# Second MLP of a three-stage kernel: a cast deferred into the next group, last blocks of the first MLP pulled forward, weight conversion reordered

## The chip, the cores and the metric

One core of one Trainium2 chip runs the whole program. The metric is device time in microseconds of one execution; the profile shows a single execution of it, engine by engine: PE (TensorE matmul), PEld (its weight loads), DVE (VectorE), ACT (ScalarE), POOL (GpSimd) and SP (SyncE, which issues most DMAs).

## The reference, cut to what matters

```python
x = retention(q, k, v, lam)          # (1536, 512): 2 x 768 tokens
h = x @ moe_w_in                     # 512 -> 2048
g = maximum(h, 0) + alpha * minimum(h, 0)
x = g @ moe_w_out                    # 2048 -> 512
h = x @ moe2_w_in
g = maximum(h, 0) ** 2
out = g @ moe2_w_out
```

All of it is float32. The kernel splits every factor into a high part that the fast matmul format holds exactly and a low rest, and forms each product as three matmuls: rest by high, high by rest, high by high.

## The kernel before, in words

Three stages follow each other: the retention, the first MLP, and the second MLP. The change touches the second MLP and the conversion of its weights, which starts inside the first.

**Second MLP, first product.** It goes in 16 groups (`GROUPS`), each a half `u` of the tokens (768) by a pair `p` of feature blocks (256 features). A group's `h` is a 2 x 2 block product, done by Strassen's scheme (Winograd's form) with seven products of half size. Here they are called product 1 to product 7, in the order in which `strassen` calls `product`; each is six matmuls of 384 columns (line 487). Their sums live in two PSUM banks, `px` and `py`, and what is used twice is copied by ACT on the way:

- after product 1, line 513 copies `px` into `py`, and product 2 accumulates on the copy;
- after product 2, line 520 copies `py` to memory (`u2`), before product 4 goes on top of it;
- after product 3, lines 500 and 501 (ACT, DVE) square the positive part: a quarter of `g`; product 5 then starts in that bank;
- after product 4, line 528 copies `py` (`u3`), before product 6 goes on top;
- after product 5, line 535 (DVE) adds `u3`, before product 7 goes on top of `px`;
- after product 6, lines 500 and 501 finish the first half of `g`; `halves` casts it (505, ACT) and takes the rest (506, DVE): this is `ga`;
- after product 7, lines 544 and 547 (DVE) finish the second half, and `halves` makes `gb` of it, again by 505 and 506.

The next group takes the same two banks in exchanged roles, so its line 513 also has to wait until line 544 has read the old `px`.

**Second MLP, second product.** `outputs2` makes six items for each group, three on `ga` and three on `gb`, of six matmuls each (line 566), into six banks that accumulate over the groups of a half. `strassen` runs the items of the group before between its own products, by `other()`: two after product 1, and one after products 3, 4, 6 and 7. In group 0 there is no group before: the items there are eight blocks (`second_block`, three matmuls each, line 280), the last two steps of the first MLP. After each of the last four blocks DVE adds an earlier partial sum (line 301), which also frees the bank.

**Conversion of the weights.** The weights come as 64-bit floats. `convert_pairs` is a generator over 16 pieces, two for each `p`; piece `k` (1024 numbers in a row) is brought to float32 by integer operations: `start` (343 and 344, ACT), then on DVE a shift (371), the sign (374), the sum (379, after which the raw words are free and the transfers of piece k+2 are issued by SP, line 331), for a first-matrix piece four more sums (388 to 392), then the cast to the high part (398, ACT) and the rest (`lows`, 359, DVE, two instructions). `start(k)` claims the block `bit` that piece k-2 held, which is free once `lows(k-2)` is done. `fill` draws from this generator, for so many microseconds of planned cost (`FILL`), at five places of a group: `fill(FILL[0])` behind line 513, then one behind each of 501, 528, 535, and the last at the end of the group. `split_x` makes the parts of `x` for a half in the same way (411, 420, 427, 429).

Nothing reorders the instructions: on each engine they stand as the code emits them, so the places of `fill` and `other` are the schedule.

Of the kernel before, what the change touches and what calls it, by code (L numbers as in the profile page):

```python
# [1 line left out]

# [113 lines left out]
def retention_then_two_mlps(  # L116
# [106 lines left out]
    def borrow(kind=F32):  # L223
        return spare[kind].pop(0)
# [92 lines left out]
    def taken(span, at, n):  # L317
        while (block := mem.claim(span, at, n)) is None:
            yield None
        return block  # L320

    def convert_pairs():

        raw, bit, done = {}, {}, {}

        def load(k):
            if k < len(pieces):
                half, p = pieces[k]
                raw[k] = yield from taken(LOW, RAW + 8 * (k % 2), 8)
                for e in range(2):  # L330
                    nc.sync.dma_start(
                        raw[k].view(U32)[:, 2 * e * DM : 2 * (e + 1) * DM],
                        w2[2 * (2 * p + e) + half],
                    )

        def start(k):
            if k < len(pieces):
                half, p = pieces[k]
                bit[k] = yield from taken(LOW, BIT + 7 * half, 4 if half else 7)
                both = raw[k].view(U32, 2)  # L340
                low, high = both[:, :, 0], both[:, :, 1]
                x = bit[k].view(F32)[:, 0 : 2 * DM]
                nc.scalar.activation(x, high.bitcast(F32), AF.Copy, scale=REBIAS)  # L343
                nc.scalar.activation(low.bitcast(I32), low, AF.Copy, scale=2.0**-29)

        def cuts(k):
            half, p = pieces[k]
            x, b = bit[k].view(F32), done[k]
            if half:
                for e in range(2):  # L350
                    yield x[:, e * DM : (e + 1) * DM], b[e].ap, b[2 + e].ap
            else:
                for c in slice(0, 2 * DM), slice(2 * DM, None):
                    yield x[:, c], b[0].ap[:, c], b[1].ap[:, c]

        def lows(k):
            if k >= 0:
                for x, hi, lo in cuts(k):
                    nc.vector.tensor_tensor(lo, x, hi.bitcast(F32), ALU.subtract)
                    yield 0.7 if pieces[k][0] else 1.2  # L360
                bit.pop(k).free()
                pairs[pieces[k]] = done.pop(k)

        yield from load(0)
        yield from load(1)
        yield 0
        yield from start(0)
        for k, (half, p) in enumerate(pieces):
            both = raw[k].view(U32, 2)
            x = bit[k].view(U32)[:, 0 : 2 * DM]  # L370
            nc.vector.tensor_scalar(x, x, 3, None, ALU.logical_shift_left)
            yield 0.7
            yield from lows(k - 1)
            nc.vector.scalar_tensor_tensor(
                x, both[:, :, 1], 0x80000000, x, ALU.bitwise_and, ALU.bitwise_or
            )
            yield 1.2
            x = x.bitcast(I32)
            nc.vector.tensor_tensor(x, x, both[:, :, 0].bitcast(I32), ALU.add)
            yield 1.2  # L380
            raw.pop(k).free()
            yield from load(k + 2)
            yield from start(k + 1)
            if half == 0:
                a11, a12, a21, a22, s1, s2, s4 = (
                    bit[k].view(F32)[:, i * DM // 2 : (i + 1) * DM // 2] for i in range(7)
                )
                nc.vector.tensor_tensor(s1, a21, a22, ALU.add)
                nc.vector.tensor_tensor(s2, s1, a11, ALU.subtract)
                yield 0.8  # L390
                nc.vector.tensor_tensor(a21, a11, a21, ALU.subtract)
                nc.vector.tensor_tensor(s4, a12, s2, ALU.subtract)
                yield 0.8
            done[k] = []
            for span, at in PAIRS_AT[p % 4][2] if half else PAIRS_AT[p % 4][0:2]:
                done[k].append((yield from taken(span, at, 2 if half else 7)))
            for x, hi, lo in cuts(k):
                nc.scalar.copy(hi, x)
        yield from lows(len(pieces) - 1)
# [52 lines left out]
    def fill(us):  # L452
        for gen in list(fillers):
            while us > 0:
                cost = next(gen, "end")
                if cost == "end":
                    fillers.remove(gen)
                if cost is None or cost == "end":
                    break
                us -= cost  # L460
# [11 lines left out]
    ends = [n for n, (u, p) in enumerate(GROUPS) if n + 1 == len(GROUPS) or GROUPS[n + 1][0] != u]  # L472
    begins = [0] + [n + 1 for n in ends[:-1]]

    def strassen(n, items):

        u, p = GROUPS[n]
        v = sum(b <= n for b in begins) - 1
        banks = (n % 2,), (1 - n % 2,)
        def product(ps, i, start=False):  # L480
            name, a = WANTED[i]
            xh, xl = (x.view(F32R, HALF) for x in need(x_parts, (v, name), makers["x", v]))
            wh, wl = (w.view(F32R) for w in need(pairs, (0, p), makers["w"]))
            for c in range(2):
                cols = slice((2 * a + c) * 128, (2 * a + c + 1) * 128)
                for j, (w, x) in enumerate(((wl, xh), (wh, xl), (wh, xh))):
                    nc.tensor.matmul(  # L487
                        ps, w[:, cols], x[:, c, :], start=start and c == 0 and j == 0,
                        stop=c == 1 and j == 2, skip_group_check=True,
                    )  # L490
            if n in ends:
                release(x_parts.pop((v, name)))

        def other():
            item = next(items, None)
            if item is not None:
                item()

        def relu_square(out, ps):
            nc.scalar.activation(out, ps, AF.Relu)  # L500
            nc.vector.scalar_tensor_tensor(out, ps, 0.0, out, ALU.max, ALU.mult)  # L501

        def halves(block):
            hi, lo = borrow(F32R), borrow(F32R)
            nc.scalar.copy(hi.view(F32R), block.view(F32))  # L505
            nc.vector.tensor_tensor(lo.view(F32R), block.view(F32), hi.view(F32), ALU.subtract)  # L506
            spare[F32].append(block)
            return hi, lo

        px = bank(f"p1_{n}", banks[0])[:, 0:HALF]  # L510
        product(px, 0, True)
        py = bank(f"p6_{n}", banks[1])[:, 0:HALF]
        nc.scalar.copy(py, px)  # L513
        fill(FILL[0])
        other()
        other()
        product(py, 1)
        us = borrow()
        u2, u3 = (us.view(F32, HALF)[:, i] for i in range(2))
        nc.scalar.copy(u2, py)  # L520
        product(px, 2)
        first_half = borrow()
        g = first_half.view(F32, HALF)
        relu_square(g[:, 0], px)
        fill(FILL[1])
        other()
        product(py, 3)
        nc.scalar.copy(u3, py)
        fill(FILL[2])
        other()  # L530
        px = bank(f"p5_{n}", banks[0])[:, 0:HALF]
        product(px, 4, True)
        second_half = borrow()
        h = second_half.view(F32, HALF)
        nc.vector.tensor_tensor(h[:, 1], px, u3, ALU.add)
        fill(FILL[3])
        product(py, 5)
        relu_square(g[:, 1], py)
        ga = halves(first_half)
        other()  # L540
        product(px, 6)
        if n == visits[p][-1]:
            release(pairs.pop((0, p)))
        nc.vector.tensor_tensor(h[:, 0], px, u2, ALU.add)
        spare[F32].append(us)
        h = second_half.view(F32)
        nc.vector.scalar_tensor_tensor(h, h, 0.0, h, ALU.max, ALU.mult)  # L547
        gb = halves(second_half)
        fill(FILL[4])
        other()  # L550
        return ga, gb

    def outputs2(n, gs):

# [359 lines left out]
    items = last_blocks()  # L914
    for n in range(len(GROUPS)):
        if n + 2 in begins:
            v = begins.index(n + 2)
            makers["x", v] = split_x(v)
            fillers.insert(0, makers["x", v])
        if n == ends[-1]:  # L920
            for j in range(BLOCKS):
                p2[j] = mem.claim(LOW, RAW + 2 * j, 2)
                nc.sync.dma_start(p2[j].view(F32), sums2[j])
        gs = strassen(n, items)
        for item in items:
            item()
        items = outputs2(n, gs)
    for item in items:
        item()

# [59 lines left out]
```

## Time and profile before

| | us |
|---|---|
| runs of the kernel before: median (lowest to highest) | 585.05 (584.18 to 585.37) |
| the profiled execution | 584.18 |
| its span, first to last instruction | 582.1 |
| PE busy | 565.3 (97%) |
| DVE busy | 380.3 (65%) |
| ACT busy | 308.9 (53%) |
| mean granted share of TensorE's clock | 0.997 |

PE's busy time counts overlapped matmuls once, and its complement is what PE stood still. The second MLP begins in the trace at 308.92 us, with product 1 of group 0, and lasts to the end.

### The profile page before, as it was taken

How to read it: one execution, taken by the hardware profiler on the slowest of the kernel's cores; microseconds unless marked ns; L12 is line 12 of the kernel's file. 1: busy time of each engine (PE TensorE's matmuls, PEld its weight loads, DVE VectorE, ACT ScalarE, POOL GpSimd, SP SyncE). 2: the span in 40 equal slices, each digit the busy share in tenths (PEclk: the TensorE clock that was granted, in tenths of full speed). 3: DMA queues.
4: the chain of work that ended last, by engine and by line, in shares of the span. 5: the costliest groups of instructions: out<-in, count | busy, mean ns of one | idle time of the engine just before them, and what ended most of it. 6: DMA issues, size and time to landing. Idle time of an engine off the chain costs nothing.

```text
span 582.1 us, 8021 instructions
## 1 busy us (share of the span) xinstructions
PE 565.3 (97%) x3154; PEld 485.4 (83%) x3154; DVE 380.3 (65%) x552; ACT 308.9 (53%) x506; POOL 34.1 (6%) x34
## 2 busy tenths in 40 slices
PE   8999999999999999999999799999999999999997
PEld 8887888888888888888888688878888888888986
DVE  3897866666576666887576676746687775652235
ACT  2666875775746667667466354355454543453221
POOL 2794000000000000000000000000000000000000
PEclk9999999999999999999999899999999999999999
DMA  7992342422632352425801442022023500023002
GB/s 262 392 391 81 109 149 105 144 78 104 217 117 100 108 193 100 169 82 180 289 1 45 151 177 100 0 73 74 36 80 138 180 1 1 0 91 127 1 0 109
DMA packets 30149, 69.22 MB, mean 119 GB/s; under 512 B 3224, under 2 KB 7328, under 8 KB 30112
## 3 DMA queue, kind: packets, MB, share of 16 engines
q1 hardware_dynamic: 26512, 55.60, 26.7%
q10 hardware_dynamic: 3600, 13.11, 6.8%
q8 instruction: 25, 0.41, 0.3%
q14 instruction: 12, 0.10, 0.0%
HBM read 56.63 MB, written 12.07 MB: 118 GB/s over the span
## 4 chain that ended last, share of the span: by engine, by line
PE 82%; DVE 7%; ACT 5%; DMA 3%; issue 2%; SPq 0%; DVEq 0%
PE h L234 22%; PE acc L280 22%; PE acc L566 17%; PE p L487 16%; PE o L763 2%; PE o L771 2%; ACT low_r_mem L505 1%; PE s L726 1%; DMA q<-in_qt_dram 1%; ACT low_r_mem L427 1%; DVE high_mem L547 1%; DVE low_r_mem L506 1%; ACT low_mem L343 1%; PE pk L786 1%; DMA r<-in_kr_dram 1%
## 5 line engine op out<-in xcount | busy, mean ns | idle before, releaser
L566 PE MATMUL acc<-high_r_mem,low_r_mem 128*128 128x512 f32 x288 | 73.8, 398 | 4.0 <-DVE high_mem L301 4.0
L566 PE MATMUL acc<-low_r_mem 128*128 128x512 f32 x288 | 73.0, 393 | 0.0
L280 PE MATMUL acc<-low_r_mem,high_r_mem 128*128 128x512 f32 x288 | 69.8, 390 | 0.0
L280 PE MATMUL acc<-low_r_mem 128*128 128x512 f32 x288 | 69.3, 389 | 0.0
L234 PE MATMUL h<-low_r_mem,high_r_mem 128*128 128x512 f32 x288 | 69.2, 389 | 0.0
L234 PE MATMUL h<-low_r_mem 128*128 128x512 f32 x288 | 69.0, 390 | 0.0
L566 PEld LDWEIGHTS acc<-high_r_mem,low_r_mem 128*128 128x128 f32 x288 | 54.2, 190 | 13.8 <-DVE high_mem L301 4.4
L234 PEld LDWEIGHTS h<-low_r_mem 128*128 128x128 f32 x288 | 54.0, 188 | 11.4 <-issue 0.2
L280 PEld LDWEIGHTS acc<-low_r_mem 128*128 128x128 f32 x288 | 54.0, 188 | 11.4 <-DVE high_mem L301 0.2
L234 PEld LDWEIGHTS h<-low_r_mem,high_r_mem 128*128 128x128 f32 x288 | 54.1, 188 | 11.2
L251 DVE SCALAR_TENSOR_TENSOR high_mem<-h,high_mem 128x512 f32<-128x512 f32 x44 | 30.3, 690 | 50.5 <-ACT high_mem L250 50.5
L280 PEld LDWEIGHTS acc<-low_r_mem,high_r_mem 128*128 128x128 f32 x288 | 54.0, 188 | 10.9
L566 PEld LDWEIGHTS acc<-low_r_mem 128*128 128x128 f32 x288 | 53.4, 188 | 9.0
L487 PE MATMUL p<-low_r_mem,high_r_mem 128*128 128x384 f32 x288 | 55.7, 337 | 3.6 <-ACT p L513 3.6
L487 PE MATMUL p<-low_r_mem 128*128 128x384 f32 x288 | 55.9, 337 | 1.6 <-ACT p L513 1.6
L487 PEld LDWEIGHTS p<-low_r_mem,high_r_mem 128*128 128x128 f32 x288 | 50.9, 188 | 7.4 <-ACT p L513 4.8
L256 ACT CAST low_r_mem<-high_mem 128x512 fp32r<-128x512 f32 x48 | 29.8, 621 | 51.4 <-DVE high_mem L251 38.3
L487 PEld LDWEIGHTS p<-low_r_mem 128*128 128x128 f32 x288 | 51.3, 189 | 5.3 <-ACT p L513 2.4
L505 ACT CAST low_r_mem<-high_mem 128x768 fp32r<-128x768 f32 x32 | 26.7, 835 | 51.8 <-DVE high_mem L547 39.4
L506 DVE TENSOR_TENSOR low_r_mem<-high_mem,low_r_mem 128x768 fp32r<-128x768 f32 x32 | 30.7, 958 | 28.9 <-ACT low_r_mem L505 28.9
L261 DVE TENSOR_TENSOR low_r_mem<-high_mem,low_r_mem 128x512 fp32r<-128x512 f32 x48 | 33.2, 693 | 16.2 <-ACT low_r_mem L256 13.7
L501 DVE SCALAR_TENSOR_TENSOR high_mem<-p,high_mem 128x384 f32<-128x384 f32 x32 | 17.8, 556 | 39.2 <-ACT high_mem L500 39.2
(97 smaller groups left out, 726.9 us busy)
## 6 DMA issues: line engine op xcount, KB each, us to landing
low_mem<-in_w_dram SPq DMA_DIRECT2D x39, 512.0 KB, 4.1
low_mem<-in_w_dram ACTq DMA_DIRECT2D x25, 512.0 KB, 3.3
sums<-high_mem SPq DMA_DIRECT2D x22, 256.0 KB, 2.2
high_mem<-xs SPq DMA_DIRECT2D x12, 384.0 KB, 5.8
high_mem<-sums SPq DMA_DIRECT2D x16, 256.0 KB, 5.3
k<-in_kt_dram SPq DMA_DIRECT2D x12, 256.0 KB, 5.7
q<-in_qt_dram SPq DMA_DIRECT2D x12, 256.0 KB, 5.1
v<-in_vr_dram SPq DMA_DIRECT2D x12, 256.0 KB, 5.7
```

What stands on the lines that cost most here:

```text
L234: nc.tensor.matmul(ph, w[:, cols], x[:, c, :], start=c == 0 and i == 0, stop=c == NC - 1 and i == 2)
L251: nc.vector.scalar_tensor_tensor(g, ph, 0.0, g, ALU.max, ALU.subtract)
L256: nc.scalar.copy(gh.view(F32R)[:, 0:TT], g)
L261: nc.vector.tensor_tensor(gl.view(F32R)[:, 0:TT], g.view(F32)[:, 0:TT], gh.view(F32)[:, 0:TT], ALU.subtract)
L280: nc.tensor.matmul(acc[t][i], w[:, cols], g, start=f == part[0] and j == 0, stop=f == part[-1] and j == 2,)
L487: nc.tensor.matmul(ps, w[:, cols], x[:, c, :], start=start and c == 0 and j == 0, stop=c == 1 and j == 2, skip_group_check=True,)
L501: nc.vector.scalar_tensor_tensor(out, ps, 0.0, out, ALU.max, ALU.mult)
L505: nc.scalar.copy(hi.view(F32R), block.view(F32))
L506: nc.vector.tensor_tensor(lo.view(F32R), block.view(F32), hi.view(F32), ALU.subtract)
L566: nc.tensor.matmul(acc2[j], g[:, e, rows], w, start=n in begins and e == 0 and i == 0, stop=n in ends and e == 1 and i == 2,)
L763: nc.tensor.matmul(po[t * D : (t + 1) * D, a, :], v_t[:, 2 * a + t, :], sc[:, t, a, :], start=a == 0, stop=c == 0, skip_group_check=True,)
L771: nc.tensor.matmul(po[d, a, :], state[b, c % 2][d, a, :], q_t[d, a, :], start=False, stop=True, skip_group_check=True,)
```

## The change

Three parts, none of which adds or takes away an instruction.

- **gb later.** `halves(second_half)` is no longer called at the end of a group; it is put on a list and called in the next group, right behind line 513's copy. The last group's runs behind the loop.
- **Blocks earlier.** In group 0 four blocks instead of two follow product 1, and two instead of one follow product 3; after product 7, and behind the group, none is left.
- **Conversion.** In `convert_pairs` the sign operation of piece k now stands ahead of `lows(k-1)` instead of behind it, and `start(k+1)` stands right behind `lows(k-1)`, ahead of the sum of piece k, instead of behind it.

```diff
@@ convert_pairs
             nc.vector.tensor_scalar(x, x, 3, None, ALU.logical_shift_left)
             yield 0.7
-            yield from lows(k - 1)
             nc.vector.scalar_tensor_tensor(
                 x, both[:, :, 1], 0x80000000, x, ALU.bitwise_and, ALU.bitwise_or
             )
             yield 1.2
+            yield from lows(k - 1)
+            yield from start(k + 1)
             x = x.bitcast(I32)
             nc.vector.tensor_tensor(x, x, both[:, :, 0].bitcast(I32), ALU.add)
             yield 1.2
             raw.pop(k).free()
             yield from load(k + 2)
-            yield from start(k + 1)
@@ strassen
-        def other():
-            item = next(items, None)
-            if item is not None:
+        def other(count=1):
+            for item in islice(items, count):
                 item()
...
         nc.scalar.copy(py, px)
+        if n > 0:
+            pending.pop()()
         fill(FILL[0])
-        other()
-        other()
+        other(2 if n > 0 else 4)
         product(py, 1)
...
         fill(FILL[1])
-        other()
+        other(1 if n > 0 else 2)
         product(py, 3)
...
-        gb = halves(second_half)
+        gs = [ga, None]
+
+        def late():
+            gs[1] = halves(second_half)
+
+        pending.append(late)
         fill(FILL[4])
         other()
-        return ga, gb
+        return gs
@@ the loop over the groups
         gs = strassen(n, items)
-        for item in items:
-            item()
         items = outputs2(n, gs)
+    pending.pop()()
     for item in items:
         item()
```

**ACT, from group 0 into group 1.** In these lists a name such as p_0 or p_1 is a bank of group 0 or 1; the change's line numbers are 1 to 3 above those of the kernel before. Before:

```order
L500 ACTIVATE high_mem<-p_0_2655 128x384
L528 COPY high_mem<-p_0_2662 128x384
L343 ACTIVATE low_mem<-low_mem 128x1024
L344 ACTIVATE low_mem<-low_mem 128x1024
L398 CAST low_r_mem<-low_mem 128x512 x2
L500 ACTIVATE high_mem<-p_0_2662 128x384
L505 CAST low_r_mem<-high_mem 128x768 x2
L513 COPY p_1_2767<-p_1_2760 128x384
L343 ACTIVATE low_mem<-low_mem 128x1024
L344 ACTIVATE low_mem<-low_mem 128x1024
```

Now:

```order
L502 ACTIVATE high_mem<-p_0_2655 128x384
L344 ACTIVATE low_mem<-low_mem 128x1024
L345 ACTIVATE low_mem<-low_mem 128x1024
L531 COPY high_mem<-p_0_2662 128x384
L399 CAST low_r_mem<-low_mem 128x512 x2
L502 ACTIVATE high_mem<-p_0_2662 128x384
L507 CAST low_r_mem<-high_mem 128x768
L344 ACTIVATE low_mem<-low_mem 128x1024
L345 ACTIVATE low_mem<-low_mem 128x1024
L515 COPY p_1_2767<-p_1_2760 128x384
L507 CAST low_r_mem<-high_mem 128x768
```

The two pairs 343/344 moved from behind to ahead of the copies 528 and 513, and the cast of `gb` (the second 505) from ahead of 513 to behind it.

**DVE, the end of group 0.** Before:

```order
L535 TENSOR_TENSOR high_mem<-p_0_2709,high_mem 128x384
L359 TENSOR_TENSOR low_r_mem<-low_mem,low_r_mem 128x512
L501 SCALAR_TENSOR_TENSOR high_mem<-p_0_2662,high_mem 128x384
L506 TENSOR_TENSOR low_r_mem<-high_mem,low_r_mem 128x768
L301 TENSOR_TENSOR high_mem<-acc_8_0_2463,high_mem 128x512
L544 TENSOR_TENSOR high_mem<-p_0_2709,high_mem 128x384
L547 SCALAR_TENSOR_TENSOR high_mem<-high_mem 128x768
L506 TENSOR_TENSOR low_r_mem<-high_mem,low_r_mem 128x768
L374 SCALAR_TENSOR_TENSOR low_mem<-low_mem 128x1024
L379 ISA low_mem<-low_mem 128x2048
L301 TENSOR_TENSOR high_mem<-acc_8_1_2464,high_mem 128x512
```

Now:

```order
L372 TENSOR_SCALAR low_mem<-low_mem 128x1024
L374 SCALAR_TENSOR_TENSOR low_mem<-low_mem 128x1024
L302 TENSOR_TENSOR high_mem<-acc_8_2_2465,high_mem 128x512
L538 TENSOR_TENSOR high_mem<-p_0_2724,high_mem 128x384
L360 TENSOR_TENSOR low_r_mem<-low_mem,low_r_mem 128x512
L503 SCALAR_TENSOR_TENSOR high_mem<-p_0_2662,high_mem 128x384
L508 TENSOR_TENSOR low_r_mem<-high_mem,low_r_mem 128x768
L302 TENSOR_TENSOR high_mem<-acc_8_3_2466,high_mem 128x512
L547 TENSOR_TENSOR high_mem<-p_0_2724,high_mem 128x384
L550 SCALAR_TENSOR_TENSOR high_mem<-high_mem 128x768
L360 TENSOR_TENSOR low_r_mem<-low_mem,low_r_mem 128x512
L381 ISA low_mem<-low_mem 128x2048
```

The sums on the banks of the blocks (301) moved from behind the sum 379 to ahead of 535 and 544 (the first two stand right above the rows shown), the sign (374) ahead of 535, and the second 359 from ahead of 501 to behind 547.

**ACT in group 9.** Before:

```order
L513 COPY p_9_3676<-p_9_3669 128x384
L520 COPY high_mem<-p_9_3676 128x384
L500 ACTIVATE high_mem<-p_9_3669 128x384
L343 ACTIVATE low_mem<-low_mem 128x1024
L344 ACTIVATE low_mem<-low_mem 128x1024
L398 CAST high_r_mem<-low_mem 128x1024
L398 CAST high_r_mem<-low_mem 128x768
L528 COPY high_mem<-p_9_3676 128x384
```

Now:

```order
L515 COPY p_9_3673<-p_9_3666 128x384
L507 CAST low_r_mem<-high_mem 128x768
L344 ACTIVATE low_mem<-low_mem 128x1024
L345 ACTIVATE low_mem<-low_mem 128x1024
L523 COPY high_mem<-p_9_3673 128x384
L502 ACTIVATE high_mem<-p_9_3666 128x384
L399 CAST high_r_mem<-low_mem 128x1024
L399 CAST high_r_mem<-low_mem 128x768
L531 COPY high_mem<-p_9_3673 128x384
```

The cast of `gb` and the pair 343/344 moved ahead of the copy 520.

## Rows read from the trace of the kernel before

**Rows 1.** The page's first part: busy time, share of the span, instructions
```profile
PE 565.3 (97%) x3154; PEld 485.4 (83%) x3154; DVE 380.3 (65%) x552; ACT 308.9 (53%) x506; POOL 34.1 (6%) x34
```
**Rows 2.** What PE waited for: total us, times, longest us
```profile
PE p L487 <- ACT p L513: 5.2, 5, 1.4
PE acc L566 <- DVE high_mem L301: 4.0, 1, 4.0
```
**Rows 3.** PE in order of time: start, us, line, tiles, count [idle before]
```profile
308.92 1.23 PE L487 MATMUL p<-low_r_mem,high_r_mem 128*128 128x384 f32 x6
...
319.78 1.31 PE L487 MATMUL p<-high_r_mem 128*128 128x384 f32 x6 [0.86 <-DVE high_mem L535]
...
323.01 1.23 PE L487 MATMUL p<-low_r_mem 128*128 128x384 f32 x6
324.08 1.55 PE L566 MATMUL acc<-high_r_mem,low_r_mem 128*128 128x512 f32 x6
329.61 2.93 PE L566 MATMUL acc<-high_r_mem,low_r_mem 128*128 128x512 f32 x6 [3.98 <-DVE high_mem L301]
...
349.61 2.38 PE L487 MATMUL p<-low_r_mem 128*128 128x384 f32 x12 [1.31 <-ACT p L513]
```
**Rows 4.** Windows of PE: stretch, length, busy (count), granted clock, DMA
```profile
326.00:329.00 3.00, 0.00 (x0) 1.00 0.00 0
...
330.00:332.00 2.00, 2.00 (x6) 0.50 0.82 301
...
349.60:351.00 1.40, 1.39 (x8) 1.00 0.51 181
```
**Rows 5.** DVE in order of time, groups 0 and 1
```profile
319.64 0.68 DVE L359 TENSOR_TENSOR low_r_mem<-low_mem,low_r_mem 128x512 fp32r<-128x512 f32 x1
...
321.69 0.96 DVE L506 TENSOR_TENSOR low_r_mem<-high_mem,low_r_mem 128x768 fp32r<-128x768 f32 x1 [0.90 <-ACT low_r_mem L505]
...
323.16 0.55 DVE L544 TENSOR_TENSOR high_mem<-p,high_mem 128x384 f32<-128x384 f32 x1
323.74 0.96 DVE L547 SCALAR_TENSOR_TENSOR high_mem<-high_mem 128x768 f32<-128x768 f32 x1
...
326.48 1.22 DVE L374 SCALAR_TENSOR_TENSOR low_mem<-low_mem 128x1024 uint32<-128x1024 uint32 x1
327.73 1.23 DVE L379 CUSTOM_DVE_ANT_0 low_mem<-low_mem 128x2048 uint16<-128x2048 uint16 x1
328.87 1.88 DVE L301 TENSOR_TENSOR high_mem<-acc,high_mem 128x512 f32<-128x512 f32 x3
```
**Rows 6.** ACT in order of time, from group 1 into group 2
```profile
345.25 0.83 ACT L505 CAST low_r_mem<-high_mem 128x768 fp32r<-128x768 f32 x1 [2.48 <-DVE high_mem L547]
345.99 1.15 ACT L343 ACTIVATE low_mem<-low_mem 128x1024 f32<-128x1024 f32 x1
347.03 1.14 ACT L344 ACTIVATE low_mem<-low_mem 128x1024 int32<-128x1024 uint32 x1
348.05 1.14 ACT L398 CAST high_r_mem<-low_mem 128x512 fp32r<-128x512 f32 x2
349.08 0.48 ACT L513 COPY p<-p 128x384 f32<-128x384 f32 x1
```
**Rows 7.** PE and ACT in order of time, group 9 (it begins at 458.68)
```profile
458.68 1.21 PE L487 MATMUL p<-low_r_mem 128*128 128x384 f32 x6
459.72 2.92 PE L566 MATMUL acc<-high_r_mem,low_r_mem 128*128 128x512 f32 x12
462.49 2.27 PE L487 MATMUL p<-low_r_mem 128*128 128x384 f32 x12
...
468.41 2.36 PE L487 MATMUL p<-low_r_mem 128*128 128x384 f32 x12
...
468.90 0.49 ACT L528 COPY high_mem<-p 128x384 f32<-128x384 f32 x1
```
**Rows 8.** The transfers of raw weights, line 331
```profile
DMA to landing us min/median/max: 3.2/3.9/5.1
```

More of the change, by code (lines that the diff above doesn't have):

```diff
@@ L1 @@
 from contextlib import ExitStack
+from itertools import islice
 import concourse.bass as bass
@@ L473, in retention_then_two_mlps @@
     begins = [0] + [n + 1 for n in ends[:-1]]
+    pending = []
     def strassen(n, items):
```

## The prediction

> **What bounds the kernel now.** I read the shares of busy time first: PE is busy for 97% of the span [rows 1], so the time is PE's work, which the change leaves alone, plus the pauses between. Then PE's waits. In the second MLP two kinds weigh most [rows 2]: five waits of 5.2 us in all for the copy 513, and one of 4.0 us for the sums 301. Third comes PE in order of time, which also shows a wait of 0.86 us for the sum 535 in group 0 [rows 3]. With the tails and the clock that are priced below, this change can win some 13 us at most.
>
> What an unhindered group looks like is in [rows 7]: a product takes 1.05 us (twelve matmuls from 468.41, two products, last 2.1 start to start) and an item 1.39 (459.72 to 462.49 for two). A group is seven and six of these, 15.6 us. I write +t for t us after its product 1 begins. PE wants product 2 at +3.8, product 4 at +7.3, product 6 at +10.8, product 7 at +13.2, the next group at +15.6.
>
> **What the removed waits cost.** The wait for 301: behind product 1 of group 1 the first item runs at 324.08, the second only at 329.61, when the second of the four 301s has ended. Three of them stood in DVE's queue behind 374 and 379, up to 328.87 [rows 3, 5]. That is 3.98 idle. TensorE's clock had then fallen: it stands at 0.50 in 330 to 332, the lower of its two levels (1.2 GHz), after a stretch without one matmul [rows 4]. The six matmuls at 329.61 took 2.93 us, the six at 324.08 took 1.55, so the clock cost 1.4. Each pause also hides 0.15 us of modelled tail (459.72 + 2.92 lies that far past 462.49 [rows 7]). Together 5.5.
>
> The five waits for 513: in [rows 6] the cast of gb (505) can't begin before 345.25, because it waits for 547; then 343, 344 and two 398 pass, and 513 starts at 349.08, PE 0.05 behind its end [rows 3]. Besides the idle time each costs the 0.15 tail and 0.1 of a slow restart (twelve matmuls 2.38 against 2.27 [rows 3, 7]): 5.2 + 5 x 0.25 = 6.5. The total that can go is **12.0**.
>
> **Part one, gb later.** 513 has no 505 in front of it any more. The two casts cost the same where they stand now, and the items that need gb come only after product 4 of the next group, 7 us later; on DVE 506 moves with it. At the boundaries where `fill` leaves nothing between, 513 was early enough (PE wants its result at +3.8, and it can start at +1.3), so nothing is won there. At the five it has gone: nothing but work that is ready stands in front of it, and I count all 6.5, then subtract what part three puts there.
>
> **Part two, blocks earlier.** Two 301s come right after 379 of group 0, the third ahead of 535 and the fourth ahead of 544. All banks are free long before group 1's second item. The 5.5 go.
>
> **Part three, conversion.** No instruction is added, but 343 and 344, 2.2 us on ACT less an overlap of 0.1, now start only when the second 359 of piece k-1 has given its block free, and whatever stands behind them on ACT waits too. What waits is what PE needs: 528, 513 or 500. I followed both queues through every group with the durations of [rows 5, 6] (an instruction that is ready starts 0.1 before the end of the one ahead of it, one that waits for another engine 0.03 behind it).
>
> - *Group 0* starts at 308.92 as before, PE alone setting that. Product 4 ends at 317.3. The second 359 (768 wide, 0.95) stands behind 501 now and ends at 317.0; 343, 344, 528 follow, to 319.6; product 6 was due at 319.0: 0.6 lost. DVE does 379, two 301, 371, 374, the third 301, and 535 ends at 322.15: product 7 waits 0.8. Before, its wait cost 1.1 with the tail. Group 1 begins at 323.25 instead of 323.01 [rows 3]: **+0.25**.
> - *Group 1.* 505 for ga ends at 324.1, 506 at 325.1, and the first item's third matmul, due at 324.75, needs it: **+0.35**. DVE goes on: fourth 301 to 325.7, 544 to 326.1, 547 to 327.1, 359 to 327.7. Only now 343 starts; 344 ends at 329.9, 513 at 330.3. PE is there at 327.4: a wait of 2.9, with its restart **+3.0**. Product 2 starts at 330.3, not 332.34.
> - *Group 5:* 359 ends at +8.05, 343 and 344 at +10.25, 528 at +10.65: just in time.
> - *Group 6:* the pair of 359 behind 501 ends at +8.4, 344 at +10.6, 528 at +11.0: **+0.3**.
> - *Group 7* runs two pieces. Its second 343 needs words whose transfer is issued after 379 of the same group ends at +8.35. They land 3.2 to 5.1 later [rows 8]; I take 4.7 for the later of the two, as it is issued behind the other. Then 343 and 344 to +15.3, 500 and 501 to +16.3, where product 1 of group 8 was due at +15.6; the following 505 and 506 hold up the first item by 0.3: **+1.1**. The bounds are 0 (3.2) and 1.5 (5.1).
> - *Group 9:* 359, 343 and 344 come ahead of 520 and shift 500, 501, the four small sums and both 398; 528, which ended at 469.39, just before PE wanted it at 469.46 (468.41 plus a product) [rows 7], ends at +11.45, due at +10.75: **+0.8**.
> - *First MLP:* the pair 343/344 comes one activation earlier at two places and delays it by about 1 us. PE has no wait there in its list, and a step's result is used two steps later, over 5 us on: nothing. SP's queue there and in groups 0 to 8 holds the same transfers; only where two pieces run in one group is the landing late, group 7.
> - Groups 2 to 4, 8 and 10 to 15 come out without a wait. At the boundaries into 4 and 12 513 waits only for 544, 1.7 us before it is due.
>
> Sum of the new: 0.25 + 0.35 + 3.0 + 0.3 + 1.1 + 0.8 = 5.8. Net 12.0 - 5.8 = **6.2 us won**. The profiled execution took 584.18, its span 582.1; the change's like execution should take 578.0. The median before is 0.87 above that execution, so the median forecast is 585.05 - 6.2 = **578.8**. Any one of these waits is the difference of two long queues, good to perhaps 0.5 us; six of them and the unknown landing make 3 us either way of the sum.
>
> **Rivals.**
>
> *The clock falls again.* The wait of 2.9 in group 1 lies between those of 1.4, after which the clock stayed at 1.00, and that of 3.98, after which it was at 0.50 [rows 4]. If it falls, the 1.4 comes back: 580.2. In length it is nearer to 3.98; but in that long pause the row 326 to 329 still reads 1.00 after three empty microseconds, so a pause of 2.9 was over before the clock moved there, and I take no fall as likelier. The Trainium skill (TensorE: Matmul & The Clock Gate, What's actually happening) says that the throttled state is the default and only activity lifts it, so that every long pause is followed by slow matmuls; our row at 330 agrees, and by that rule alone the sum would be 4.8 won instead of 6.2. Chance 0.14.
>
> *All pauses go.* If 343 finds its block free earlier than I reckon, because DVE gets to 359 between its waits, group 1 loses little and 12 us are won but for a few tenths: 573 to 576. Against it stands that 359 is behind 547 on an engine that keeps its order, and 547 needs product 7. Chance 0.08.
>
> *Slower: ACT's head of the line.* 343 waits for a late transfer or a late 359 with 528, 513 or 500 behind it, in groups 0, 1, 5, 6, 7 and 9. I reckon 5.8 for these. If 343 starts 1.5 us later than I have it at all six, 9 us more are lost, 2.8 more than are won: 587.9, and 589.3 with the clock's 1.4 in group 1. It turns to slower from 1.0 us later at all six (6.2 / 6). For it: in group 5 there is only 0.1 to spare, and group 7 hangs on a landing of 3.2 to 5.1. Against it: the others hang on DVE instructions whose durations vary by hundredths. Chance 0.05.
>
> *It does nothing.* The pauses move on into the same groups and cancel: 584 to 586. That needs as much new waiting as old, twice what I count. Chance 0.05.
>
> **How the numbers follow.** The forecast as worked out has 0.68. No change means within 0.2%, 1.2 us, about what a measurement of this kernel can tell from none. Faster: 0.68 + 0.14 + 0.08 = 0.90; the same 0.05; slower 0.05. The range takes the forecast with its 3 us and the clock's case: 575.8 to 582.0; it leaves out most of the case without pauses, and the last two.
>
> **What would show it.** PE's waits should have no 301 left, and a single one for 513 of any size, 2.9 at about 327.4 to 330.3, with 343 and 344 right ahead of 513 on ACT and the second 359 right ahead of 343. There should be short waits for 528 in groups 0, 6 and 9, one for 535 in group 0, and one of 0.7 at the start of group 8, with the second 343 of group 7 released by a transfer. The windows 330 to 333 should show a granted clock of 1.00. PE's busy time should fall by the slow matmuls alone, 1.5 us at most. Wrong would be: a 513 that waits in more groups than one, 513 free in group 1, a clock of 0.50 in the second MLP, or pauses in the first.

## The result, and the profile after

The change takes 579.13 us (median of four runs, 578.02 to 579.38), the kernel before 584.79 in the same comparison (four runs, 584.18 to 585.37). The ratio is 0.9900, interval 0.9883 to 0.9917: 5.7 us faster, where 6.2 were forecast, and inside the range. The profiled execution took 579.38, its span 577.3. One per cent of the time before is 5.85 us; kernels of different comparisons are set beside each other below by their ratios.

The lines of the changed kernel stand one to eight further down than before: 343, 344 are now 344, 345; 359 is 360; 379 is 381; 301 is 302; 500 and 501 are 502 and 503; 505 and 506 are 507 and 508; 513, 520, 528, 535 are 515, 523, 531, 538; 544 and 547 are 547 and 550; 566 is 574; 280 is 281 and 487 is 490. In the experiments they differ again, by up to nine.

The page's first part, after; PE is as busy as before [rows 1]:

```profile
PE 565.1 (98%) x3154; PEld 485.5 (84%) x3154; DVE 379.3 (66%) x552; ACT 309.6 (54%) x506; POOL 33.9 (6%) x34
```

What PE waited for, the rows of the second MLP (total us, times, longest):

```profile
PE p L490 <- ACT p L515: 2.7, 1, 2.7
...
PE p L490 <- DVE high_mem L538: 1.4, 1, 1.4
...
PE p L490 <- DVE high_mem L503: 0.3, 1, 0.3
PE p L490 <- ACT high_mem L531: 0.2, 1, 0.2
```

Beside [rows 2]: the wait of 4.0 for the block sums is gone, and of five waits for the copy one is left, 2.7 long.

PE in order of time, from the end of group 0 (as [rows 3] before):

```profile
322.73 1.32 PE L490 MATMUL p<-high_r_mem 128*128 128x384 f32 x6 [1.36 <-DVE high_mem L538]
323.88 1.23 PE L490 MATMUL p<-low_r_mem 128*128 128x384 f32 x6
324.95 3.28 PE L574 MATMUL acc<-high_r_mem,low_r_mem 128*128 128x512 f32 x12
330.92 3.28 PE L490 MATMUL p<-low_r_mem 128*128 128x384 f32 x12 [2.69 <-ACT p L515]
334.00 2.24 PE L574 MATMUL acc<-high_r_mem,low_r_mem 128*128 128x512 f32 x6
```

Both items of group 1 now run one behind the other from 324.95 (3.28 for twelve matmuls against 2.92 [rows 7]: 0.36 is lost inside them), and product 2 starts at 330.92 (332.34 before). But the twelve matmuls of products 2 and 3 took 3.28, not 2.27 [rows 7], and the six of the next item 2.24 instead of 1.55. The windows of PE over this stretch (as [rows 4]) show why:

```profile
328.30:330.90 2.60, 0.00 (x0) 1.00 0.18 39
330.90:332.00 1.10, 1.08 (x6) 1.00 0.95 357
332.00:335.50 3.50, 3.50 (x12) 0.51 0.42 163
335.50:337.00 1.50, 1.50 (x9) 1.00 0.00 0
```

PE stood from 328.3 to 330.9 with the clock at 1.00, resumed at full speed, and only after a microsecond of work did the clock go to 0.5, its lower level of 1.2 GHz.

The chain that made the wait, DVE and then ACT in order of time (as [rows 5] and [rows 6]):

```profile
325.52 0.68 DVE L302 TENSOR_TENSOR high_mem<-acc,high_mem 128x512 f32<-128x512 f32 x1
326.12 0.55 DVE L547 TENSOR_TENSOR high_mem<-p,high_mem 128x384 f32<-128x384 f32 x1
326.71 0.96 DVE L550 SCALAR_TENSOR_TENSOR high_mem<-high_mem 128x768 f32<-128x768 f32 x1
327.58 0.69 DVE L360 TENSOR_TENSOR low_r_mem<-low_mem,low_r_mem 128x512 fp32r<-128x512 f32 x1
```

```profile
315.86 1.14 ACT L344 ACTIVATE low_mem<-low_mem 128x1024 f32<-128x1024 f32 x1
...
328.35 1.15 ACT L344 ACTIVATE low_mem<-low_mem 128x1024 f32<-128x1024 f32 x1 [3.73 <-DVE low_r_mem L360]
329.39 1.10 ACT L345 ACTIVATE low_mem<-low_mem 128x1024 int32<-128x1024 uint32 x1
330.38 0.49 ACT L515 COPY p<-p 128x384 f32<-128x384 f32 x1
```

The copy 515 is ready when 547 has ended, at 326.67, but stands behind 344 and 345, which wait for the rest 360, which stands behind 550. It ends 4.2 us later.

### The profile page after: what moved, and what is told of

Same layout as the page of the kernel before. It is cut to its first block, busy times and chain, and to the rows that moved or that the text cites. A ratio compares the mean times of both kernels' runs of the same rounds, so it can differ in the third digit from the quotient of the medians.

```text
span 577.3 us, 8029 instructions
## 1 busy us (share of the span) xinstructions
PE 565.1 (98%) x3154; PEld 485.5 (84%) x3154; DVE 379.3 (66%) x552; ACT 309.6 (54%) x506; POOL 33.9 (6%) x34
## 4 chain that ended last, share of the span: by engine, by line
PE 85%; DVE 5%; ACT 4%; DMA 4%; issue 1%; SPq 0%; ACTq 0%; DVEq 0%
PE h L235 23%; PE acc L281 22%; PE acc L574 19%; PE p L490 16%; PE o L771 2%; PE o L779 2%; PE s L734 1%; DMA q<-in_qt_dram 1%; ACT low_mem L344 1%; ACT low_mem L345 1%; PE pk L794 1%; DMA r<-in_kr_dram 1%; DMA zd<-z 1%; DMA low_mem<-in_w_dram 1%; DVE low_r_mem L360 1%
## 5 line engine op out<-in xcount | busy, mean ns | idle before, releaser
L250 ACT ACTIVATE high_mem<-h 128x512 f32<-128x512 f32 x44 | 26.2, 596 | 31.7 <-PE h L235 31.7
```

The costliest lines, as they stand in the source:

```text
L250: nc.scalar.activation(g, ph, AF.Relu, scale=-1.0)
```

## The experiments

Two questions: do the waits for 513 come from the cast of gb (theory one), or from where the conversion stands (theory two)? And does the wait that is left in group 1 come from the late rest ahead of the pair 344/345, or from something else?

**Each part alone, and one and two together.** The edits are the hunks of the diff: gb later; blocks earlier (the counts of `other`); conversion (order of sign, rests, start, sum).

> Only the first part: gb's cast behind the next group's copy 513; blocks and conversion as before. Theory one (the cast of gb in front of 513 is what made PE wait for 513): four of the five waits for 513 go (into groups 2, 4, 5, 12); the one into group 8 stays at about 0.8, because the pair 343/344 ahead of 513 then waits for its transfer. The wait for 301 shrinks from 3.98 to about 2, because 506 of gb no longer stands ahead of it on DVE. Time 576 to 577. Theory two (it is the conversion that frees 513): each wait for 513 shrinks by one cast, 0.8, and about 3 us are won: 581 to 582.

Measured: 575.76 (574.79 to 577.06), ratio 0.9844 (0.9825 to 0.9862), already faster than the whole change. PE's waits in the second MLP:

```profile
PE acc L575 <- DVE high_mem L301: 2.1, 1, 2.1
...
PE p L489 <- DVE high_mem L539: 0.9, 1, 0.9
```

No wait for the copy is left in any group (0.8 was expected into group 8), and the one for the block sums fell from 4.0 to 2.1 as well. Before, the rest of gb and its wait for the cast had stood on DVE ahead of 374, 379 and the sums [rows 5]:

```profile
325.60 0.96 DVE L506 TENSOR_TENSOR low_r_mem<-high_mem,low_r_mem 128x768 fp32r<-128x768 f32 x1 [0.90 <-ACT low_r_mem L505]
```

Both, 0.90 and 0.96, are gone from there. Part one alone wins 1.56% or 9.1 us.

> Only the second part: first MLP's last blocks earlier in group 0. Both theories: the wait for 301 and the slow clock behind it go (5.5 us). Theory one: all five waits for 513 stay (5.2 us), and a new one of about 0.6 comes into group 1, since gb's cast stands ahead of 513 there and 301 no longer covers it; the wait for 535 in group 0 grows from 0.9 to about 1.5. Time 580 to 581. Theory two gives the same here, so this run prices the second part alone.

Measured: 583.73 (582.73 to 587.8), ratio 0.9984 (0.9965 to 1.0004): 0.9 us by the ratio, not to be told from none; a miss. The page has no 301 wait, but:

```profile
PE p L488 <- ACT p L513: 7.2, 6, 2.6
```

The longest stands in front of product 2 of group 2. ACT's copy there, and PE behind it:

```profile
347.83 0.47 ACT L513 COPY p<-p 128x384 f32<-128x384 f32 x1
```

```profile
348.35 1.86 PE L488 MATMUL p<-low_r_mem 128*128 128x384 f32 x9 [2.65 <-ACT p L513]
```

Before, that copy started at 349.08 [rows 6]: 1.3 later, while the pause of group 1 was 4.0. PE arrives earlier and ACT nearly as late as before; what was removed in group 1 had been cover for the ACT queue at the start of group 2, whose wait grew from 1.31 [rows 3] to 2.65. A new one of 0.7 stands in group 1.

> Only the third part: the rests of the converted weights behind the sign, the next piece's start ahead of the sum. Theory one: of the waits for 513 those into groups 2 and 8 go or shrink, those into 4, 5 and 12 stay (no 343/344 stood ahead of them), the wait for 301 stays at about 3.4 with the slow clock, and new waits for 528 in groups 6 and 9 and at the start of group 8 come. Net about 1 us: 583.5 to 584.5. Theory two (the conversion brings most of the gain): 579 to 581.

Measured: 585.63 (582.99 to 586.51), ratio 0.9999 (0.9985 to 1.0012). Nothing is won: 513 waits three times for 3.0 in all, two fewer, but

```profile
PE p L487 <- ACT high_mem L520: 0.8, 2, 0.6
PE p L487 <- ACT high_mem L528: 0.5, 1, 0.5
PE p L487 <- DVE high_mem L501: 0.4, 1, 0.4
```

came in their place, and the wait for 301 is still 3.3. Theory two falls.

> The first and second part without the third. Theory one (the third part only costs: 2.7 us and the slow clock in group 1, 0.4 in group 6, 0.9 into group 8, 0.3 in group 9): the wait of 2.7 for 513 in group 1 is gone with the slow clock, since 343/344 stand behind 513 there again; left are 535 in group 0 (about 1.5), a short wait for 506 in group 1, and one of about 0.8 for 513 into group 8. Time 574 to 575, some 5 us below the whole change. Theory two (the conversion is what frees 513): the waits into groups 2 and 8 stay, and the time is 581 or more.

Measured: 573.6 (572.53 to 574.36), ratio 0.9801 (0.9783 to 0.9818): 11.6 us faster than before and 5.8 faster than the whole change. One row of the second MLP is left:

```profile
PE p L490 <- DVE high_mem L538: 1.4, 1, 1.4
```

So the wait for 538 in group 0 belongs to part two (it puts 302 ahead of 538), not to part three, and part three costs the change 5.8 us. The waits that it brings, 2.95 in group 1, 0.4, 0.9 and 0.35 in groups 6 to 9, and 1.5 of slow clock make 6.1.

In the profiled executions the second MLP doesn't begin at the same time: between 308.5 and 310.7, in e7 below at 312.2. So about a microsecond of a difference in the whole time can lie ahead of it. From its first product to the end it took 273.2 us before, 268.0 in the change, 265.1 in e1, 270.7 in e2, 271.7 in e3 and 261.9 in e4. That is 2.5 less than before in e2 and 1.5 less in e3, of which 1.4 is the clock, which fell in the execution before and not in theirs; so parts two and three are worth little alone by this measure too. The change takes 6.0 more than e4.

**What in part three costs.** Four edits take it apart.

```diff
             nc.vector.scalar_tensor_tensor(
                 x, both[:, :, 1], 0x80000000, x, ALU.bitwise_and, ALU.bitwise_or
             )
             yield 1.2
             yield from lows(k - 1)
-            yield from start(k + 1)
...
             yield from load(k + 2)
+            yield from start(k + 1)
```

(against the whole change)

> Parts one and two, and of part three only its first half: the sign operation ahead of the rests, the start of the next piece left behind the sum. Theory one (the cost of part three is the start moved ahead on ACT): no different from parts one and two alone, 573.6 within 0.8, no wait for 515 in the second MLP. Theory two (the cost is the rests, which come one operation later on DVE and hold the block): a wait for 515 of 1 to 2.7 us in group 1 and a total of 575 to 579.

Measured: 573.68 (573.0 to 574.17), ratio 0.9795 (0.9773 to 0.9816), the same as parts one and two. Later rests alone cost nothing; the start has to come forward as well.

```diff
             yield from lows(k - 1)
+            yield from start(k + 1)
             nc.vector.scalar_tensor_tensor(
                 x, both[:, :, 1], 0x80000000, x, ALU.bitwise_and, ALU.bitwise_or
             )
...
             yield from load(k + 2)
-            yield from start(k + 1)
```

(against parts one and two)

> Parts one and two, and of part three only its second half: the start of the next piece right behind the rests and ahead of sign and sum, the rests in their old place. ACT then has the order of the whole change, but the pair 344/345 at the end of group 0 no longer waits for a rest that stands behind 550. Theory one (a pair ahead of 515 costs by its wait for a late rest, not by its 2.2 us alone): the wait in group 1 is under 1 us, no fall of the clock there, total 573.5 to 575.5. Theory two (the pair ahead of 515, 531 and 523 costs by its own length wherever it stands): the wait in group 1 stays at 2 us or more, total 577 to 579.

Measured: 585.95 (583.78 to 587.19), ratio 1.0003 (0.9988 to 1.0018): all that was won is lost, and both expectations missed. PE's waits, and ACT in group 1:

```profile
PE p L490 <- ACT p L515: 4.4, 2, 3.7
PE acc L281 <- DVE high_mem L302: 3.0, 2, 1.9
```

```profile
331.96 1.13 ACT L344 ACTIVATE low_mem<-low_mem 128x1024 f32<-128x1024 f32 x1 [4.80 <-DMA low_mem<-in_w_dram]
```

The pair no longer waits for a rest, as meant, but for its raw words: issued 11.3 us behind the start of group 0, where the change has 10.9, the two transfers took 7.2 and 8.0 us instead of 3.5 and 4.9. Why they were slow the trace doesn't tell. In the first MLP two pauses of 3.0 in all appeared, which the change doesn't have. The profiled execution is the fastest of twelve; the others have mean clocks down to 0.988, so part of the median's loss is the clock. So this run does not separate the two explanations; the next does.

```diff
+        fill(0.7 if n == 0 else 0)
         nc.vector.tensor_tensor(h[:, 0], px, u2, ALU.add)
...
-        fill(FILL[4])
+        fill(FILL[4] if n > 0 else 0.8)
```

(against the change; it moves one DVE instruction, ACT stands as it was)

> The change with one instruction moved: the second rest (360) at the end of group 0 stands ahead of 547 on DVE instead of behind 550; ACT's order is untouched, 344 and 345 still stand ahead of 515. Theory one (the 2.7 us in group 1 are the pair's wait for that rest): 360 ends some 1.3 us or more earlier, the pair with it, the wait for 515 falls from 2.7 to between 0.7 and 1.4, no fall of the clock, total 576 to 577.2. Theory two (the pair costs by its own length, or 515 waits for 547): the wait stays at 2.5 or grows, as 547 now stands behind 360, total 579 or more.

Measured: 576.92 (576.33 to 577.63), ratio 0.9852 (0.9835 to 0.987), 2.8 us better than the change. ACT, and PE behind it:

```profile
326.67 1.16 ACT L344 ACTIVATE low_mem<-low_mem 128x1024 f32<-128x1024 f32 x1 [2.27 <-DVE low_r_mem L360]
327.73 1.16 ACT L345 ACTIVATE low_mem<-low_mem 128x1024 int32<-128x1024 uint32 x1
328.77 0.49 ACT L515 COPY p<-p 128x384 f32<-128x384 f32 x1
```

```profile
329.32 2.35 PE L490 MATMUL p<-low_r_mem 128*128 128x384 f32 x12 [1.31 <-ACT p L515]
```

The rest came earlier, the pair with it, and the wait halved; 547 was pushed back by it and it didn't matter. The twelve matmuls took 2.35 where the change's took 3.28: no slow clock. The 1.31 that is left comes of the pair's place: the copy, ready at 327.06 when 547's sum ended, stood behind the pair until 328.77, and PE had stopped at 328.00. A rest that comes earlier still was not tried. So about half of the wait was the late rest, as theory one says, and the other half the pair itself.

```diff
-        fill(FILL[4])
+        fill(FILL[4] if n > 0 else 0)
```

(against the change)

> The change with one edit: nothing is drawn from the conversion at the end of group 0, so that the second rest (line 360), the sum 381 and the pair 344/345 of that place come later, behind the copy 515 of group 1. Theory one (the 2.7 us wait in group 1 comes from the pair 344/345, which waits for the rest behind 550 and stands ahead of 515; the slow clock after it comes from that pause): the wait of 2.7 and the fall of the clock both go, about 4 us won against the change, 575 to 576, less whatever the pair costs where it stands next (ahead of the 515 of group 2: up to 2 us). Theory two (515 in group 1 is late through PE's own order or DVE's 547, whatever ACT does in between): the wait stays, 579.

Measured: 577.93 (576.85 to 578.77), ratio 0.9873 (0.9848 to 0.9898), 1.6 us better than the change by the ratios, whose intervals overlap; theory one's 575 to 576 is missed. The wait for 515 and the slow clock are gone, and the pair stands in front of the next copy, 523, instead:

```profile
PE p L490 <- ACT high_mem L523: 1.1, 1, 1.1
...
PE p L490 <- ACT high_mem L531: 0.7, 2, 0.6
```

**The parts in pairs.** Part three with one of the others.

> Parts one and three without two. Theory one (part three costs some 5 us wherever part one stands, in group 1 and in groups 6 to 9): the 301 pause stays as well as the pair's wait, 579 to 583. Theory two (part three costs only together with the blocks moved in part two, since these make group 0 denser): no dearer than part one alone, 575 to 577.

Measured: 575.8 (574.85 to 577.32), ratio 0.9834 (0.9814 to 0.9855): theory two's figure. Part three costs nothing beside part one alone (0.9844). The rows show it; ACT's copy and PE in group 1:

```profile
328.62 0.51 ACT L515 COPY p<-p 128x384 f32<-128x384 f32 x1
```

```profile
322.09 2.24 PE L280 MATMUL acc<-low_r_mem,high_r_mem 128*128 128x512 f32 x9
324.17 1.23 PE L489 MATMUL p<-low_r_mem 128*128 128x384 f32 x6
...
328.26 1.66 PE L575 MATMUL acc<-high_r_mem,low_r_mem 128*128 128x512 f32 x6 [1.47 <-DVE high_mem L301]
329.75 2.27 PE L489 MATMUL p<-low_r_mem 128*128 128x384 f32 x12
```

Without part two, three blocks still run between product 7 and group 1, and under them part of the chain from 547 to the copy: the copy ends 5.0 us behind the group's start at 324.17, not 7.0 as in the change. And 301 holds PE until 328.26; the item behind it lasts until 329.75, longer than the copy, which ended at 329.13. Of two late things in one place only the longer costs here.

> Parts two and three without one. Theory one (the gain of the change is part one's): no faster than before by more than 3 us, 582 to 587. Theory two (the three parts need each other and the conversion takes the pairs away from the copies): faster than part two alone, 581 or less.

Measured: 588.2 (587.57 to 589.56), ratio 1.0047 (1.0031 to 1.0063), slower than before, and above the 582 to 587 of theory one. The cast of gb and the late pair both stand ahead of 513, with no 301 to hide them:

```profile
PE p L488 <- ACT p L513: 7.6, 4, 4.6
```

**The last wait of parts one and two.**

```diff
-        fill(FILL[2])
+        fill(FILL[2] if n > 0 else 0)
```

(against parts one and two)

> Parts one and two, with one edit: in group 0 nothing is drawn from the conversion between products 4 and 5 (FILL[2]), so that DVE reaches 538 earlier. Theory one (the 1.4 us wait for 538 in group 0 is DVE's queue of conversion work ahead of it): that wait shrinks to under 0.4, total 572.2 to 573.0. Theory two (it is the third and fourth of the sums 302, which part two puts ahead of 538, or the rest of the conversion comes back as a wait for 515 or 506 in group 1): 573.6 or more.

Measured: 572.86 (572.6 to 573.64), ratio 0.9784 (0.9763 to 0.9805). The wait for 538 is gone; one of 0.7 for 531 came in group 1, where the conversion now stands. The three sums 302 still stand ahead of 538 in this run, so they don't make that wait without the conversion's instructions between them. It is the fastest kernel found, 12.6 us under the one before, though its interval overlaps that of parts one and two alone.

## Why the prediction was right, point by point

- **What the old waits cost, 12.0: right.** Parts one and two alone won 11.6. What they bring on their own (the longer wait for 538 in group 0 and 0.35 for the first item's third matmul) is what the prediction's groups 0 and 1 name.
- **Which part removes what: wrong.** The prediction gave 6.5 to part one and 5.5 to part two. Alone they won 9.1 and 0.9; only together do they come to its sum. The step that failed is to count each part's waits as that part's alone. Part one also takes 1.9 from the wait for 301, by way of DVE (e1). And "The 5.5 go" holds only with part one in place: a pause that is removed brings PE sooner to the next late thing, in e2 the ACT queue at the start of group 2.
- **Group 1, +3.0: right.** 547, 550, 360, 344, 345, 515 came in the order forecast, each 0.6 later than given, as the group itself began 0.6 later (323.88 for 323.25, of which 0.42 because group 0 began at 309.34 and not at 308.92; the copy ended at 330.87 for 330.3). Moving that one rest (e9) halved the wait.
- **Group 0, +0.25: wrong in its reason.** 528 was to lose 0.6 because 343 waits for the second 359. It didn't: 344 started at 315.86 with no wait, and the second rest only later, at 316.47 in DVE's order. That block is a first-matrix piece; the pair writes its first 1024 numbers, which the first rest has read (argued from `start` and the rows, not tried alone). PE then met 538 earlier and waited 1.36 instead of the 0.8 forecast. Group 5, "just in time", had 1.7 us to spare for the same reason (its copy ended at 400.48, product 6 began at 402.2). The first MLP has no new pause, as forecast.
- **Groups 6, 7/8 and 9.** Forecast 0.3, 1.1, 0.8. The trace has waits of 0.16, 0.27 with 0.08 for the first item, and 0.08, which with restarts make 0.4, 0.9 and 0.35. The second pair of group 7 was released by a transfer, as named:

```profile
436.06 1.13 ACT L344 ACTIVATE low_mem<-low_mem 128x1024 f32<-128x1024 f32 x1 [2.83 <-DMA low_mem<-in_w_dram]
```

  Its words had landed 4.4 after the first of the two transfers was issued, where 4.7 was taken. In group 9 the copy 531 ended 0.5 earlier in the group than worked out.
- **The clock: the rival, with a chance of 0.14, held in most runs.** A clock of 0.50 in the second MLP, which the prediction named as a sign of being wrong, came. I took the clock to stay up after 2.9 us, because [rows 4] show 1.00 through a stretch of empty time. It fell in three of four executions (mean clock 0.997; 578.97 to 579.38; where, only the profiled one shows); in the fourth the mean was 1.00 and the time 578.02, beside the 578.0 worked out without a fall. In the profiled execution the slow matmuls cost 1.5, and PE's busy time fell by 0.2 alone. The failed step is reading "the clock hasn't moved yet" as "it won't": in the windows above it fell after PE had resumed.
- **The sum.** The terms added by the profiled rows come to 0.5 + 0.35 + 2.95 + 0.4 + 0.9 + 0.35 = 5.45 (5.8 forecast), and the clock's 1.5 on top: 12.0 less these is 5.05 won, and the second MLP of the profiled executions is 5.2 shorter. Their whole times, 584.18 and 579.38, are 4.8 apart, so the profiled execution is 1.4 slower than the 578.0 forecast for it. The median comes within 0.3 of its forecast because here the profiled execution is the highest of four, where before it was the lowest. That closeness is in part luck.

## What to carry to other kernels

Put what is ready on an in-order queue ahead of what may wait: a pair of activations that waits for a late rest costs more than its own 2.2 us, because everything behind it waits as well, here the copy that PE needs. Pauses at one place cost the longest of them (e10), so a part that costs nothing alone (e3) or beside one other (e10) can cost 5.8 us once another part has taken the cover away, and a removed pause (e2) may return in the next queue; try the parts alone and in pairs before crediting them. Here two of three parts were worth more than all three.

## What the runs showed of the hardware that was not expected

The length of a pause didn't decide whether TensorE's clock fell. It fell after 2.12 us in e1, where the windows before, at and after the resumption read:

```profile
325.00:327.20 2.20, 0.22 (x1) 1.00 0.00 0
327.30:328.40 1.10, 1.07 (x4) 0.86 0.24 91
328.60:331.50 2.90, 2.90 (x10) 0.50 1.03 314
```

It didn't after 2.65 in e2 and 3.33 in e3, whose windows over the pause and behind it read:

```profile
345.70:348.30 2.60, 0.00 (x1) 1.00 1.03 375
348.40:352.00 3.60, 3.60 (x19) 1.00 0.27 99
```

```profile
326.10:329.40 3.30, 0.03 (x1) 1.00 0.00 0
329.50:333.00 3.50, 3.50 (x18) 1.00 0.78 265
```

The change itself went both ways from run to run. So in a forecast a pause of 2 to 4 us should carry the slow clock as a chance, not as a yes or no. The Trainium skill (TensorE: Matmul & The Clock Gate, What's actually happening) says that the monitor's window runs freely and isn't reset when the kernel starts. That one kernel goes both ways agrees with it; no run here shows the window itself.

In the profiled executions the pauses that were followed by a fall were of 2.12 (e1), 2.69 (the change), 3.75 (e7), 3.98 (before) and 4.57 us (e11). That doesn't make shorter ones safe. Of the 48 executions of the kernel before that stand beside the experiments, 26 have a mean clock of 0.994 or 0.991, two and three times the loss of the one fall in its profile (0.997), although that profile has only one pause above 1.4 us. Which pauses did it there, no trace shows.
